# A DiT block on one core: summing the MLP gate over partition quadrants by small DMAs and VectorE in place of float32 matmuls between the fc1 panels

## The chip, the cores and the metric

The kernel runs on one core of one Trainium2 chip. The metric is device time in microseconds (us) of one execution. Each execution comes with the span of the core (first to last instruction; about 1.8 us less than the time) and the mean clock that the throttle granted TensorE. One execution of each kernel is profiled; its trace gives every instruction's start and duration.

## The reference

```python
B, N, D = 2, 256, 1152          # F = 4 * D, two heads
mod = (silu(c) @ w_mod).reshape(B, 6, 1, D)
shift_a, scale_a, gate_a, shift_m, scale_m, gate_m = [mod[:, i] for i in range(6)]
h = layernorm(x) * (1 + scale_a) + shift_a
...                                             # attention
x = x + gate_a * a
h2 = layernorm(x) * (1 + scale_m) + shift_m
m = gelu(h2 @ w_fc1) @ w_fc2
return x + gate_m * m
```

All inputs are bf16. The part that matters is the last line: `gate_m` is a vector of 1152 numbers for each of two batches, silu(c) times a 1152 x 1152 slice of `w_mod`, and it is needed only when fc2's results leave PSUM, the memory into which TensorE writes its sums.

## The kernel before

TensorE is the busy engine, so the kernel computes `gate_m` on VectorE. The rows of the weight slice lie on 128 partitions in 9 chunks; VectorE multiplies and adds the chunks, transposes 32x32 blocks and sums them. That leaves `folded`, whose 128 partitions are 4 quadrants of 32, still to be summed. The kernel before does this last sum with one float32 matmul for each batch against `fold`, which is four 32x32 identity matrices stacked. The two matmuls are issued on TensorE between the fc1 panels 34 and 35 (the last).

```python
fold = const.tile([P, 32], FP32, name="fold")
nc.vector.tensor_reduce(fold[:], ident[:].rearrange("p (q a) -> p a q", a=32), axis=AX.X, op=ALU.add)
# ...
def gate_vector(g, wg):
    # ... 18 passes of VectorE over 128 x 1152 make part
    for b in range(B):
        for c in range(0, D, PW):
            blocks = work.tile([P, PW // 32, 32], FP32, name="tmp", tag="tmp", bufs=3)
            nc.vector.transpose(blocks[:].rearrange("p j r -> p (j r)"), part[:, b, c:c + PW])
            nc.vector.tensor_reduce(folded[:, b, c // 32:(c + PW) // 32], blocks[:], axis=AX.X, op=ALU.add)
    return lambda: gate_vector_finish(g, folded)

def gate_vector_finish(g, folded):
    rows = D // 32
    pg = aux_tile([rows, B, 32], "pg")                       # PSUM
    for b in range(B):
        nc.tensor.matmul(pg[:, b, :], folded[:, b, :], fold[:], start=True, stop=True)
    nat = work.tile([rows, B, 32], BF16, name="nat_v", tag="nat_v", bufs=1)
    nc.vector.tensor_copy(nat[:], pg[:])
    for b in range(B):
        nc.gpsimd.dma_start(gates_dram[g, b, :].rearrange("(j r) -> j r", r=32), nat[:, b, :])
    return broadcast_gate(g)                                 # two DMAs: DRAM row -> all 128 partitions
# ... fc1, the panels of 128 columns of F from 12 on:
for m in range(MSPLIT, KF):                                  # MSPLIT = 12, KF = 36
    pacc = acc_tile([P, T], "pacc")                          # T = 512 tokens
    for k in range(KD):                                      # KD = 9
        f1_mm(pacc[:], m, k, 0, T, k == 0)
    nc.scalar.activation(gT[:, m, :], pacc[:], ACT.Gelu_apprx_tanh)
    if m == 22:
        gate_m_finish = gate_vector(1, w_gate_m)
    if m == KF - 2:
        gate_m = gate_m_finish()
    # ... fc2 weight loads
# ... fc2, 13 groups of 36 matmuls; each group's result is multiplied by the gate:
    nc.vector.tensor_tensor(tmp[:], pacc[:], gate_m[:, b, c0:c0 + cw], op=ALU.mult)
```

At the head, TensorE runs float32 matmuls on zeros only to warm up, `warm(2, pwarm)` and `warm(7, pwarm)`, until the first normalized rows of x arrive from VectorE (`norm1`).

## Time and profile before

| | before |
|---|---|
| time, median of three runs | 242.99 us (242.89 to 243.03) |
| span of the profiled execution | 241.3 us |
| TensorE matmul busy | 236.3 us, 98% |
| VectorE busy | 91.6 us, 38% |
| granted clock | 1.000 |

From the page of the kernel before, its first part (busy us, share of the span, count) and the split by engine of the chain that ended last (the waits and the work, followed back from the last instruction; a name with q is an engine's sequencer, and "issue" is time for which the profile shows no wait):

```profile
span 241.3 us, 3993 instructions
PE 236.3 (98%) x1698; PEld 144.6 (60%) x1698; DVE 91.6 (38%) x194; ACT 60.1 (25%) x122; POOL 28.3 (12%) x47
...
PE 95%; DMA 2%; DVE 1%; SPq 0%; issue 0%; DVEq 0%
```

TensorE is busy nearly all the time, and the chain of work that ended last runs on it for 95% of the span. So only what takes time away from TensorE, or makes it wait, changes the time.

The chain of the kernel before in order of time (start us, us, what):

```profile
1.63 4.60 DMA x_sb<-in_x_dram
...
9.37 0.53 PE pm L250 x18
...
97.31 68.26 PE pacc L750 x423
165.57 0.26 PE pg L491 x4
165.82 2.05 PE pacc L750 x9
167.87 70.31 PE pacc L806 x468
```

L750 is fc1, L806 is fc2. From 97.31 us on TensorE never waits. The gate appears in this chain for 0.26 us only, as pg. From the start of fc1 to the start of fc2 it is 167.87 - 97.31 = 70.56 us.

How long does pg hold TensorE up? From the timeline of the kernel before (start us, us, engine, line, operation; in brackets the idle time before it and who ended it):

```profile
163.66 0.60 ACT L782 ACTIVATE gT<-pacc 128x512 bf16<-128x512 f32 x1 [1.34 <-PE pacc L750]
165.50 0.21 PEld L491 LDWEIGHTS pg<-fold,folded 128*36 128x36 f32 x4 [0.42 <-issue]
165.50 0.33 PE L491 MATMUL pg<-fold,folded 128*36 128x32 f32 x4
165.61 0.60 ACT L782 ACTIVATE gT<-pacc 128x512 bf16<-128x512 f32 x1 [1.35 <-PE pacc L750]
165.76 2.12 PE L750 MATMUL pacc<-hT,w_f 128*128 128x512 bf16 x9
167.91 0.60 ACT L782 ACTIVATE gT<-pacc 128x512 bf16<-128x512 f32 x1 [1.71 <-PE pacc L750]
```

The Gelu of each panel starts when the panel is complete. Undisturbed panels follow each other at 1.94 us (163.66 to 165.61 within rounding); the last one takes 2.30 us. The difference of 0.36 us is what the two float32 matmuls (four passes) cost, with whatever they disturb around them.

### The profile page before, as it was taken

Reading aid. Unit: us, or ns where it says so; the run is one execution under the profiler, and the core shown is the slowest. Engines: PE = TensorE matmul, PEld = TensorE weight load, DVE = VectorE, ACT = ScalarE, POOL = GpSimd, SP = SyncE. Lnnn points to the kernel's source line nnn. Section 1 sums busy time; section 2 is a strip of 40 time slices with the busy share of each in tenths; the row PEclk is TensorE's granted clock in tenths of the full one; section 3 lists DMA queues with packets and bytes.
Section 4 is the critical chain, followed back from the end, with each engine's and each line's share of the span. In section 5 each row is a group of like instructions: output and inputs, shape, how many; then the busy total and the mean of one; then the engine's idle time right before and its main releaser. Section 6 shows DMA issues by size and latency. Waiting matters only on the chain.

```text
span 241.3 us, 3993 instructions
## 1 busy us (share of the span) xinstructions
PE 236.3 (98%) x1698; PEld 144.6 (60%) x1698; DVE 91.6 (38%) x194; ACT 60.1 (25%) x122; POOL 28.3 (12%) x47
## 2 busy tenths in 40 slices
PE   8899999999999999999999999999999999999994
PEld 5675444466667566888844444444666656666674
DVE  4842442319325678930002999950000000000001
ACT  6732322307215032770423333222000000000000
POOL 2300000001400324100000000001121111111111
PEclk9999999999999999999999999999999999999999
DMA  6999999998599994739999999999300000000000
GB/s 196 324 317 311 376 367 391 389 393 249 99 315 397 387 311 81 196 62 364 390 392 392 339 326 284 285 326 275 98 16 16 20 16 16 19 18 18 26 25 16
DMA packets 48925, 53.30 MB, mean 221 GB/s; under 512 B 9731, under 2 KB 36619, under 8 KB 48907
## 3 DMA queue, kind: packets, MB, share of 16 engines
q1 hardware_dynamic: 41312, 50.14, 62.6%
q10 hardware_dynamic: 7083, 1.72, 4.9%
q0 software_dynamic: 512, 1.19, 2.2%
q8 instruction: 13, 0.21, 0.4%
q14 instruction: 5, 0.04, 0.1%
HBM read 50.15 MB, written 1.19 MB: 213 GB/s over the span
## 4 chain that ended last, share of the span: by engine, by line
PE 95%; DMA 2%; DVE 1%; SPq 0%; issue 0%; DVEq 0%
PE pacc L806 29%; PE pacc L750 29%; PE pacc L697 7%; PE pacc L603 7%; PE pq L525 7%; PE pk L282 5%; PE pk L311 2%; DMA x_sb<-in_x_dram 2%; PE pa L644 2%; PE ps_s L560 2%; PE pn L420 2%; PE pt L267 1%; PE pm L250 1%; DVE stats L195 1%; PE pg L502 0%; SPq L88 0%
## 5 line engine op out<-in xcount | busy, mean ns | idle before, releaser
L750 PE MATMUL pacc<-hT,w_f 128*128 128x256 bf16 (+1 forms) x432 | 70.5, 326 | 0.0
L806 PE MATMUL pacc<-w_f,gT 128*128 128x384 bf16 (+2 forms) x468 | 70.5, 314 | 0.0
L806 PEld LDWEIGHTS <-gT 128*128 128x128 bf16 x468 | 44.4, 98 | 26.2
L750 PEld LDWEIGHTS <-w_f 128*128 128x128 bf16 x432 | 42.2, 98 | 27.6
L812 DVE TENSOR_TENSOR tmp<-pacc,gate 128x384 f32<-128x384 f32 (+2 forms) x13 | 6.9, 527 | 65.6 <-PE pacc L806 57.3
L782 ACT ACTIVATE gT<-pacc 128x512 bf16<-128x512 f32 x24 | 14.3, 597 | 32.7 <-PE pacc L750 32.7
L473 DVE SCALAR_TENSOR_TENSOR part<-w_gate_m,s,part 128x1152 f32<-128x1152 bf16 x16 | 21.4, 1414 | 0.0
L814 POOL TENSOR_TENSOR o_sb<-tmp,x 128x384 bf16<-128x384 f32 (+1 forms) x12 | 11.6, 971 | 53.9 <-DVE tmp L812 53.9
L697 PE MATMUL pacc<-w_o,big 128*128 128x384 bf16 x108 | 17.9, 326 | 0.0
L525 PE MATMUL pq<-hT,w_q 128*128 128x512 bf16 x81 | 17.8, 379 | 0.0
L603 PE MATMUL pacc<-w_v,hT 128*128 128x384 bf16 x108 | 17.7, 326 | 0.0
L603 PEld LDWEIGHTS <-hT 128*128 128x128 bf16 x108 | 10.5, 98 | 7.1 <-issue 0.3
L697 PEld LDWEIGHTS <-big 128*128 128x128 bf16 x108 | 10.4, 98 | 7.2 <-issue 0.4
L525 PEld LDWEIGHTS <-w_q 128*128 128x128 bf16 x81 | 7.9, 98 | 9.4
L282 PE MATMUL pk<-big,w_k 128*128 128x256 bf16 (+1 forms) x72 | 13.2, 325 | 0.0
L703 POOL TENSOR_TENSOR x<-tmp,x_sb 128x384 f32<-128x384 f32 x8 | 7.3, 911 | 26.3 <-DVE tmp L702 26.3
L471 DVE TENSOR_SCALAR part<-w_gate_m,s 128x1152 f32<-128x1152 bf16 x2 | 1.6, 818 | 22.2 <-DMA w_gate_m<-in_w_mod_dram 22.2
L495 POOL DMA_DIRECT2D gates_dram<-nat_v x2 | 1.1, 534 | 67.7 <-DVE nat_v L493 67.7
L282 PEld LDWEIGHTS <-w_k 128*128 128x128 bf16 x72 | 6.8, 97 | 3.5 <-issue 0.2
L771 ACT ACTIVATE gT<-pacc 128x512 bf16<-128x512 f32 x12 | 6.5, 597 | 9.1 <-PE pacc L750 9.1
L516 POOL DMA_DIRECT2D gates_dram<-nat x4 | 2.4, 596 | 49.8 <-DVE nat L513 48.4
L175 PE MATMUL pwarm<-zeros 128*128 128x256 f32 x18 | 6.7, 540 | 1.2 <-DVE eps_t L95 1.2
(106 smaller groups left out, 164.4 us busy)
## 6 DMA issues: line engine op xcount, KB each, us to landing
w_f<-in_w_fc_dram SPq DMA_DIRECT2D x12, 864.0 KB, 14.2
w_f<-in_w_fc_dram SPq DMA_DIRECT2D x3, 1728.0 KB, 10.1
w_f<-in_w_fc_dram SPq DMA_DIRECT2D x2, 2592.0 KB, 17.2
w_gate_a<-in_w_mod_dram SPq DMA_DIRECT2D x3, 864.0 KB, 14.4
w_v<-in_wqkv_dram SPq DMA_DIRECT2D x3, 864.0 KB, 15.4
w_o<-in_wo_dram SPq DMA_DIRECT2D x3, 864.0 KB, 14.7
w_shift_m<-in_w_mod_dram SPq DMA_DIRECT2D x3, 864.0 KB, 9.5
w_scale_m<-in_w_mod_dram SPq DMA_DIRECT2D x3, 864.0 KB, 15.8
```

The costliest lines, as they stand in the source:

```text
L175: nc.tensor.matmul(dst[:, 0:T // 2], zeros32[:, 0:P], zeros32, start=True, stop=True)
L282: nc.tensor.matmul(pk[m][:, c0:c1], w_k[:, k, m * P:(m + 1) * P], hT0[:, k, c0:c1], start=(k == 0 and c0 == 0), stop=(k == KD - 1), skip_g ...
L473: nc.vector.scalar_tensor_tensor(part[:, b, :], wg[:, k, :], s32[:, k, b:b + 1], part[:, b, :], op0=ALU.mult, op1=ALU.add,)
L525: nc.tensor.matmul(pq[m][:], w_q[:, k, m * P:(m + 1) * P], hT[:, k, :], start=(k == 0), stop=(k == KD - 1), skip_group_check=True,)
L603: nc.tensor.matmul(pacc[:], hT[:, k, t * P:(t + 1) * P], w_v[:, k, pnl * PW:(pnl + 1) * PW], start=(k == 0), stop=(k == KD - 1),)
L697: nc.tensor.matmul(pacc[:], aT[:, k, t * P:(t + 1) * P], w_o[:, k, c0:c1], start=(k == 0), stop=(k == KD - 1),)
L703: (nc.gpsimd if pool_add else nc.vector).tensor_tensor(x1[:, t, c0:c1], tmp[:], x_sb[:, t, c0:c1], op=ALU.add)
L750: nc.tensor.matmul(dst, w_f1[m // KD][:, k, ml * P:(ml + 1) * P], hT[:, k, c0:c1], start=start, stop=(k == KD - 1), **kw,)
L782: nc.scalar.activation(gT[:, m, :], pacc[:], ACT.Gelu_apprx_tanh)
L806: nc.tensor.matmul(pacc[:], gT[:, kk, t * P:(t + 1) * P], w_f2[j][:, r, c0 - n * PW:c0 - n * PW + cw], start=(kk == 0), stop=(kk == KF - 1),)
L812: nc.vector.tensor_tensor(tmp[:], pacc[:], gate_m[:, b, c0:c0 + cw], op=ALU.mult)
L814: (nc.vector if last else nc.gpsimd).tensor_tensor(o_sb[:], tmp[:], x1[:, t, c0:c0 + cw], op=ALU.add)
```

## The change

The intent: get the two float32 matmuls off TensorE. Four small DMAs bring the four quadrants side by side on 32 partitions, VectorE sums them, transposes, and converts to bf16, and the whole follows `folded` at once, without a place in TensorE's program.

```diff
-    fold = const.tile([P, 32], FP32, name="fold")
-    nc.vector.tensor_reduce(fold[:], ident[:].rearrange("p (q a) -> p a q", a=32), axis=AX.X, op=ALU.add)
 ...
-        return lambda: gate_vector_finish(g, folded)
-
-    def gate_vector_finish(g, folded):
         rows = D // 32
-        pg = aux_tile([rows, B, 32], "pg")
-        for b in range(B):
-            nc.tensor.matmul(pg[:, b, :], folded[:, b, :], fold[:], start=True, stop=True)
-        nat = work.tile([rows, B, 32], BF16, name="nat_v", tag="nat_v", bufs=1)
-        nc.vector.tensor_copy(nat[:], pg[:])
-        for b in range(B):
-            nc.gpsimd.dma_start(gates_dram[g, b, :].rearrange("(j r) -> j r", r=32), nat[:, b, :])
+        quads = small.tile([32, P // 32, B * rows], FP32, name="quads", tag="quads", bufs=1)
+        for a in range(P // 32):
+            nc.gpsimd.dma_start(quads[:, a, :], folded[32 * a:32 * (a + 1), :, :].rearrange("p b j -> p (b j)"))
+        total = small.tile([32, 96], FP32, name="total", tag="total", bufs=1)
+        nc.vector.memset(total[:], 0.0)
+        nc.vector.tensor_reduce(total[:, 0:B * rows], quads[:].rearrange("p a c -> p c a"), axis=AX.X, op=ALU.add)
+        turned = small.tile([32, 96], FP32, name="turned", tag="turned", bufs=1)
+        nc.vector.transpose(turned[:], total[:])
+        nat = small.tile([32, 96], BF16, name="nat_v", tag="nat_v", bufs=1)
+        nc.vector.tensor_copy(nat[:], turned[:])
+        # ... two DMAs of nat to gates_dram instead of two
         return broadcast_gate(g)
 ...
         if m == 22:
-            gate_m_finish = gate_vector(1, w_gate_m)
-        if m == KF - 2:
-            gate_m = gate_m_finish()
+            gate_m = gate_vector(1, w_gate_m)
```

More of the change, by code (lines that the diff above doesn't have):

```diff
@@ L483, in gate_vector @@
                 )
-        return lambda: gate_vector_finish(g, folded)
-    def gate_vector_finish(g, folded):
         rows = D // 32
-        pg = aux_tile([rows, B, 32], "pg")
-        for b in range(B):
-            nc.tensor.matmul(pg[:, b, :], folded[:, b, :], fold[:], start=True, stop=True)
-        nat = work.tile([rows, B, 32], BF16, name="nat_v", tag="nat_v", bufs=1)
-        nc.vector.tensor_copy(nat[:], pg[:])
-        for b in range(B):
-            nc.gpsimd.dma_start(gates_dram[g, b, :].rearrange("(j r) -> j r", r=32), nat[:, b, :])
+        quads = small.tile([32, P // 32, B * rows], FP32, name="quads", tag="quads", bufs=1)
[3 more added lines that the diff above has]
+        nc.vector.memset(total[:], 0.0)
+        nc.vector.tensor_reduce(
+            total[:, 0:B * rows], quads[:].rearrange("p a c -> p c a"), axis=AX.X, op=ALU.add,
+        )
+        turned = small.tile([32, 96], FP32, name="turned", tag="turned", bufs=1)
+        nc.vector.transpose(turned[:], total[:])
+        nat = small.tile([32, 96], BF16, name="nat_v", tag="nat_v", bufs=1)
+        nc.vector.tensor_copy(nat[:], turned[:])
+        flat = gates_dram[g, :, :].rearrange("b (j r) -> (b j) r", r=32)
+        nc.gpsimd.dma_start(
+            flat[0:64, :].rearrange("(q c) r -> c q r", q=2), nat[:, 0:64].rearrange("c (q r) -> c q r", q=2),
+        )
+        nc.gpsimd.dma_start(flat[64:B * rows, :], nat[0:B * rows - 64, 64:96])
         return broadcast_gate(g)
```

## The prediction

> **What bounds the kernel now.** TensorE. The page's first part shows PE busy 236.3 of 241.3 us (98%), and the chain of waits is 95% PE. The clock is 1.000. In the fc1/fc2 stretch the chain is PE without a gap: 68.26 us of fc1 panels, then "PE pg L491 0.26 us", then 2.05 us of the last panel, then 70.31 us of fc2. So of the MLP gate only those matmuls are on the critical path.
>
> **What the change removes.** (a) The four float32 matmul passes of pg between panels 34 and 35. Two ways to cost them: the chain gives 0.26 us; the spacing of the Gelu starts is 1.94 us for every panel from 12 on, and 2.30 us (165.61 to 167.91) for the panel with pg in front of it. The difference, 0.36 us, also holds the drain and the restart of the weight loads, so I take 0.36 us. [...] a 128x36 float32 load takes 114 ns, a 128x128 bf16 load 98. (b) One VectorE reduction (fold, 0.36 us at 32.8 us), with VectorE idle 4.8 us afterwards: worth nothing.
>
> **What it adds.** The order of instructions shows nothing moved on TensorE or ScalarE. Four small DMAs on GpSimd's queue once folded is ready (160.4 us), then on VectorE a memset, a 32x288 reduction, a 32x96 transpose and a copy, then two small DMAs instead of two. Both engines are idle there, so this delays nobody.
>
> **When the gate arrives.** Before: nat_v DMAs issued at 166.4 and 166.9 (0.53 us each, landing in 3.5 to 3.8 us), broadcast from 170.8, and the first fc2 multiply starts at 174.40, waiting for that DMA. After: four issues from about 160.7 to 162.9, landing about 166 to 166.5 (the weight loads still move some 315 GB/s there); VectorE about 0.9 us (estimated from the 553 ns reduction of 384 columns and the 317 ns transpose of 128); two DMAs to about 171; broadcast to about 175.5. [...] this trace has 3.5 to 3.8, and I use the trace. The first fc2 group ends near 173.5, so its multiply waits 1 to 4 us. This is off the path: there are six PSUM accumulators and a group lasts 5.9 us, so TensorE would stall for the gate only if it came near 200 us.
>
> **Predicted time.** 242.99 - 0.36 = 242.6 us, 0.15% faster, just above the 0.14 us scatter of the three runs. Range 242.3 to 242.95. Chances: faster by over 2% 0.003, within 2% 0.994, slower 0.003.
>
> **What would show each step.** Right: no pg matmuls, 1.94 us between all the last Gelu starts, fc2 starting 0.35 us earlier (167.35 instead of 167.71), PE busy time down 0.3 us, quads landing near 166, first fc2 multiply at 174 to 177.5 with a wait for the gate DMA, no wait of PE in fc2. Wrong: an fc2 matmul waiting for VectorE; a shift of the fc1 start (97.1 us).
>
> **What would make it wrong.** Small DMAs stuck behind the weight loads for over 20 us; a lower granted clock; a shift in the first 30 us, where DMA bounds the kernel, from other placement of tiles or semaphores, which would hide a gain of this size.

Two clauses are cut where marked; no term of the sum went with them, and 242.99 - 0.36 = 242.6 us stands.

## The result, and the profile after

| | before | after |
|---|---|---|
| six executions each, median | 243.01 us (242.89 to 243.35) | 243.32 us (242.89 to 244.04) |
| ratio, after over before | | 1.0013, 95% interval 0.9997 to 1.0028 |
| span of the profiled execution | 241.3 us | 241.4 us |
| start of fc1 to start of fc2, from the chain | 70.56 us | 70.20 us |

A ratio here is the mean time of one kernel's runs over that of the other's runs of the same rounds; it is not quite the ratio of the medians. Executions over 1.5% slower than the fastest of the same kernel are left out of the means.

Within 2%, as forecast. But the time lies above the forecast range, and if anything the change looks slower. The page of the changed kernel, the same lines:

```profile
span 241.4 us, 3993 instructions
PE 235.1 (97%) x1694; PEld 144.0 (60%) x1694; DVE 92.2 (38%) x196; ACT 60.2 (25%) x122; POOL 30.3 (13%) x51
...
PE 95%; DMA 3%; SPq 1%; DVE 0%; issue 0%; DVEq 0%
```

TensorE has four matmul passes fewer and is busy 1.2 us less (0.3 was forecast), yet the span is 0.1 us longer. The busy time says little of the gain here: 0.8 of the 1.2 us is the warming at the head, which ended at 7.14 us and not at 7.95. The chain of the changed kernel (L755 is fc1 now, L809 fc2):

```profile
2.58 7.20 DMA w_scale_a<-in_w_mod_dram
...
9.82 0.60 PE pm L250 x18
...
97.80 70.20 PE pacc L755 x432
168.00 70.30 PE pacc L809 x468
```

Here is the whole result in two subtractions. From the start of fc1 to the start of fc2: 168.00 - 97.80 = 70.20 us, against 70.56, so 0.36 us less, to the last digit what was forecast. But fc1 starts at 97.80 us and not at 97.31: 0.49 us later. At the head of the chain stands another load: the first piece of w_scale_a kept TensorE waiting until 9.82 us, where in the kernel before these matmuls stand at 9.37. The change has no instruction there. The gain is real in its stage, and was lost 88 us before that stage began.

The timeline of the changed kernel around the last panels and the gate:

```profile
161.53 2.02 POOL L486 DMA_DIRECT2D quads<-folded  x4 [62.38 <-DVE total L488]
...
164.15 0.60 ACT L787 ACTIVATE gT<-pacc 128x512 bf16<-128x512 f32 x1 [1.35 <-PE pacc L755]
166.09 0.60 ACT L787 ACTIVATE gT<-pacc 128x512 bf16<-128x512 f32 x1 [1.34 <-PE pacc L755]
...
168.04 0.60 ACT L787 ACTIVATE gT<-pacc 128x512 bf16<-128x512 f32 x1 [1.35 <-PE pacc L755]
168.63 0.63 DVE L489 TENSOR_REDUCE total<-quads 32x72 f32<-32x288 f32 x1 [7.30 <-DMA quads<-folded]
...
175.69 0.56 DVE L815 TENSOR_TENSOR tmp<-pacc,gate 128x384 f32<-128x384 f32 x1 [5.89 <-DMA gate<-gates_dram]
```

The last Gelus are 1.94 us apart now, the last one too. The gate arrives at 175.69 us (174.40 before, forecast 175.5), and VectorE is idle for 5.89 us before it. The first fc2 group is complete at 173.85 us, so the gate alone accounts for 1.84 us of that, within the forecast 1 to 4. TensorE does not notice: fc2 takes 70.30 us as before.

So what has to be explained is the 0.49 us at the start. Three theories:

- S: the landing of the first loads scatters from one execution to the next, in both kernels alike; the first comparison was unlucky.
- L: the change moves something. It does: without `fold`, every large tile stands 128 bytes lower in SBUF, the on-chip memory for tiles (128 bytes a partition is the size of `fold`; the addresses were read from the built programs, which the kept traces do not show), among them the targets of the first loads.
- a third, that the cost on TensorE was misread and something else hides it.

### The profile page after: what moved, and what is told of

The parts are those of the page before. It is cut to its first block, busy times and chain, and to the rows that moved or that the text cites. A ratio compares the mean times of both kernels' runs of the same rounds, so it can differ in the third digit from the quotient of the medians.

```text
span 241.4 us, 3993 instructions
## 1 busy us (share of the span) xinstructions
PE 235.1 (97%) x1694; PEld 144.0 (60%) x1694; DVE 92.2 (38%) x196; ACT 60.2 (25%) x122; POOL 30.3 (13%) x51
## 4 chain that ended last, share of the span: by engine, by line
PE 95%; DMA 3%; SPq 1%; DVE 0%; issue 0%; DVEq 0%
PE pacc L809 29%; PE pacc L755 29%; PE pacc L702 7%; PE pacc L608 7%; PE pq L530 7%; PE pk L282 5%; DMA w_scale_a<-in_w_mod_dram 3%; PE pk L311 2%; PE pa L649 2%; PE ps_s L565 2%; PE pn L420 2%; PE pt L267 1%; PE pm L250 1%; SPq L88 1%; PE pg L507 0%
## 5 line engine op out<-in xcount | busy, mean ns | idle before, releaser
L809 PE MATMUL pacc<-w_f,gT 128*128 128x384 bf16 (+2 forms) x468 | 70.5, 314 | 0.0
L755 PE MATMUL pacc<-hT,w_f 128*128 128x256 bf16 (+1 forms) x432 | 70.4, 326 | 0.0
L809 PEld LDWEIGHTS <-gT 128*128 128x128 bf16 x468 | 44.4, 98 | 26.2
L755 PEld LDWEIGHTS <-w_f 128*128 128x128 bf16 x432 | 42.3, 98 | 27.8
L486 POOL DMA_DIRECT2D quads<-folded x4 | 2.0, 509 | 62.4 <-DVE total L488 62.4
L707 DVE TENSOR_TENSOR tmp<-pacc,gate 128x384 f32<-128x384 f32 x12 | 6.6, 549 | 3.1 <-PE pacc L702 3.1
```

The costliest lines, as they stand in the source:

```text
L707: nc.vector.tensor_tensor(tmp[:], pacc[:], gate_a[:, b, c0:c1], op=ALU.mult)
L755: nc.tensor.matmul(dst, w_f1[m // KD][:, k, ml * P:(ml + 1) * P], hT[:, k, c0:c1], start=start, stop=(k == KD - 1), **kw,)
L809: nc.tensor.matmul(pacc[:], gT[:, kk, t * P:(t + 1) * P], w_f2[j][:, r, c0 - n * PW:c0 - n * PW + cw], start=(kk == 0), stop=(kk == KF - 1),)
```

## The experiments

Eighteen runs were made, in five calls, each on another chip and with its own eleven executions of the kernel before.

### First call: repeat, move the tiles, take only the matmuls out

**e1_after_again**: the changed kernel, no edit.

> The changed kernel once more, unaltered. Theory S (scatter of the start: the landing of the first x and w_scale_a loads varies by about half a us from one execution to the next, the same in both kernels): mean of the rounds about 0.36 us under the kernel before, 242.6 to 242.9, and in its profile the fc1 start may lie anywhere from 97.2 to 97.9 us while fc1 start to fc2 start stays 70.20 us. Theory L (placement: dropping the fold tile moves every large tile by 128 bytes in SBUF, and the first loads land later for it, always): about 243.3 again, fc1 start near 97.8 us.

Measured: its profiled execution (276.94 us, mean granted clock 0.853; its clock record has 0.850 from 5.05 us to the end) is left out. The five others: 242.57 to 243.51 us, mean 242.99; the kernel before in the same rounds 243.41; ratio 0.9982 (0.9964 to 0.9999). Theory S expected a mean 0.36 us below the kernel before and got 0.42; theory L expected 243.3. So the changed kernel is not always slower. But the kernel before, measured eleven times, ran between 242.84 and 243.91: the scatter is far over the 0.14 us of the first three runs.

**e2_after_fold**: the changed kernel with `fold` back, so the large tiles stand where they stood.

```diff
+    fold = const.tile([P, 32], FP32, name="fold")
+    nc.vector.tensor_reduce(fold[:], ident[:].rearrange("p (q a) -> p a q", a=32), axis=AX.X, op=ALU.add)
```

> The changed kernel with the unused fold tile and its reduction put back, so that x_sb, w_scale_a, w_k and all large tiles stand at the addresses of the kernel before; the float32 matmuls stay away. Theory L: the start is again that of before (fc1 start 97.3 us) and the whole gain shows: 242.6 us, ratio to before 0.9985. Theory S: no different from e1_after_again within the scatter, whatever that is.

Measured: mean 242.87 us (242.62 to 242.98), ratio 0.9977 (0.9963 to 0.9991). That is 0.12 us under e1, well inside the scatter.

**e3_before_layout**: the kernel before with the large tiles where the changed kernel has them.

```diff
-    fold = const.tile([P, 32], FP32, name="fold")
+    fold = small.tile([P, 32], FP32, name="fold", tag="fold", bufs=1)
...
-        nat = work.tile([rows, B, 32], BF16, name="nat_v", tag="nat_v", bufs=1)
+        nat = small.tile([rows, B, 32], BF16, name="nat_v", tag="nat_v", bufs=1)
```

> The kernel before with fold and nat_v moved to the other pool, so that all large tiles stand at the addresses of the changed kernel; the same instructions, the float32 matmuls stay. Theory L: fc1 start near 97.8 us, 243.5 us, ratio 1.002. Theory S: as before, 243.0 us, ratio 1.000 within 0.1%.

Measured: mean 243.56 us (243.27 to 243.79) against 243.41, ratio 1.0007 (0.9991 to 1.0023). fc1 started at 97.57 us in its chain. The time itself fits what theory L had written, 243.5, but only because the kernel before was at 243.41 in these rounds too and not at 243.0; the ratio is what counts, and it is a third of the 1.002 expected. Moving the tiles down cost 0.15 us here and moving them up gained 0.12 in e2. Neither is clear of noise, and the upper end of e3's interval, 1.0023, is still 0.56 us. Taken together the two give 0.14 us with a standard error of 0.11 from the spread of their times: an effect of 0.1 us cannot be excluded, but the 0.5 us that theory L needed is unlikely. A trace speaks against it too: e7 below, which has the tiles where the kernel before has them, waited for the same piece of w_scale_a until 9.90 us, longer than the changed kernel did (9.82).

**e4_before_nopg**: the kernel before with only the matmuls gone. Its output is wrong, which doesn't matter for the time.

```diff
-        pg = aux_tile([rows, B, 32], "pg")
-        for b in range(B):
-            nc.tensor.matmul(pg[:, b, :], folded[:, b, :], fold[:], start=True, stop=True)
...
-        nc.vector.tensor_copy(nat[:], pg[:])
+        nc.vector.tensor_copy(nat[:], folded[0:rows, :, 0:32])
```

> The kernel before with only the four float32 matmul passes taken out (nat_v is copied from folded itself, so the MLP gate is wrong on purpose); layout, fold reduction and DMAs as before. Both theories, if the cost of the matmuls on TensorE was read rightly: fc1 start to fc2 start 70.20 us instead of 70.56, and 242.65 us, ratio 0.9985. If the gain is not there even so, the cost of the matmuls was misread.

Measured: mean 243.04 us (242.42 to 244.01), ratio 0.9983 (0.9962 to 1.0005). Its chain:

```profile
97.23 70.20 PE pacc L747 x432
167.43 70.30 PE pacc L803 x468
```

70.20 us again, with layout and DMAs as before. The price of the matmuls on TensorE is 0.36 us, and nothing of the added DMAs or VectorE work takes any of it back.

### What all traces agree on

The table takes each trace of a fast execution with the usual head of the program and no matmuls added, and reads five starts from it: TensorE's first matmul of the k projection, of the q projection, of fc1, of fc2, and the end. These are starts of instructions; the chain counts a piece from the end of the one before, which is some 0.16 us later.

| trace | pg on TensorE | first k | first q | first fc1 | first fc2 | end | fc1 to end |
|---|---|---|---|---|---|---|---|
| before | yes | 10.13 | 31.92 | 97.15 | 167.71 | 241.26 | 144.12 |
| e15_before_look | yes | 9.96 | 31.71 | 96.94 | 167.50 | 241.05 | 144.12 |
| e3_before_layout | yes | 10.44 | 32.17 | 97.40 | 167.97 | 241.52 | 144.12 |
| after | no | 10.64 | 32.40 | 97.64 | 167.84 | 241.39 | 143.76 |
| e12_after_third | no | 10.12 | 31.86 | 97.09 | 167.29 | 240.85 | 143.76 |
| e16_after_look | no | 9.99 | 31.70 | 96.93 | 167.13 | 240.69 | 143.76 |
| e2_after_fold | no | 10.13 | 32.19 | 97.43 | 167.63 | 241.18 | 143.75 |
| e4_before_nopg | no | 10.10 | 31.84 | 97.07 | 167.27 | 240.82 | 143.75 |
| e11_gate_late | no | 9.97 | 31.71 | 96.94 | 167.14 | 240.69 | 143.75 |

The last column has two values, 144.12 with the matmuls and 143.75 or 143.76 without. From the first q matmul to the first fc1 matmul it is 65.23 or 65.24 us in every row. All the variation is in the first 32 us: the first q matmul lies anywhere from 31.70 to 32.40 us, twice the size of the gain.

In e2_after_fold the start has a second source of delay: its k projection began as early as in the kernel before, but its chain then runs through the load of w_q:

```profile
20.29 11.85 DMA w_q<-in_wqkv_dram
32.14 0.04 issue
32.19 5.35 PE pq L532 x24
```

TensorE could not start q before that load landed.

### Second call: delay the start, multiply the cost

**e5_late_before** and **e6_late_after**: both kernels with more warming, so that TensorE comes to the first loads later.

```diff
-    warm(7, pwarm)
+    warm(14, pwarm)
```

> The kernel before with seven more warming matmuls at the head of TensorE's program, so that TensorE reaches the first projection some 3 us later, when the first x and w_scale_a tiles have landed in every execution. Theory S (the disputed sign of the change is scatter of the first landings): slower than before by 2 to 4 us, and its executions lie within about 0.3 us of each other, where those of the kernel before spread over 1.1 us; fc1 start to the end stays 144.12 us. Theory L (the placement, not scatter): the spread stays as it is.

> The changed kernel with the same seven matmuls. Theory S: 0.36 us under e5_late_before in the mean of the rounds, with little scatter, so that the gain is seen in the whole time and not only in the stage; fc1 start to the end 143.76 us. Theory L: as slow as e5_late_before or slower, since its large tiles stand 128 bytes lower.

Measured: e5 mean 244.77 us (244.27 to 245.30), e6 mean 244.75 us (244.01 to 245.32). The scatter did not shrink and the difference of the means is 0.02 us. Expectation missed. In their traces the stage still has its two values, 144.12 and 143.75 us. These runs seemed to speak against theory S; the third call showed why they could not tell.

**e7_pg12_f32**: the kernel before with twelve more pairs of float32 matmuls of pg's shape, one pair after each of twelve panels. **e8_pg12_bf16**: the same pairs in bf16.

```diff
+    px = aux_tile([36, B, 32], "px")
     for m in range(MSPLIT, KF):
 ...
+        if KF - 14 <= m < KF - 2:
+            for e in range(B):
+                nc.tensor.matmul(px[:, e, :], shift_m[:].rearrange("p k c -> p (k c)")[:, 0:36], fold[:], start=True, stop=True)
```

(in e8 the two operands are `ident[:, 0:36]` and `ident[:, 0:32]`)

> The kernel before with twelve more pairs of float32 matmuls of pg's shape, one pair after each of panels 22 to 33, results unused. If the price of one pair between two panels is 0.36 us, as the spacing of the Gelu starts says: 12 x 0.36 = 4.3 us more, about 247.4 us, ratio 1.018, and each of those panels 2.30 us instead of 1.94. If it is the 0.26 us of the chain: 3.1 us more. If the matmuls cost TensorE nothing in truth: no change.

> The same with twelve pairs of bf16 matmuls of the same shape. If the price is mostly that of float32 (four passes and slower weight loads instead of two): under half of e7_pg12_f32, about 0.1 to 0.15 us a pair, 1.2 to 1.8 us more. If it is mostly a drain of TensorE at any odd matmul between the panels: nearly as much as e7_pg12_f32.

Measured: e7 mean 247.47 us (247.15 to 247.91), ratio 1.0166; e8 mean 246.52 us (245.95 to 247.01), ratio 1.0127. The kernel before had a mean of 243.42 us in these rounds, so twelve float32 pairs cost 4.05 us of whole time (4.3 expected). In the trace of e7, fc1 to the end is 148.44 us, 4.32 us over 144.12: 0.36 us a pair. Multiplied by twelve, the cost is far above the scatter. From the timeline of e7:

```profile
163.46 0.33 PE L790 MATMUL px<-fold,shift_m 128*36 128x32 f32 x4
163.56 0.60 ACT L783 ACTIVATE gT<-pacc 128x512 bf16<-128x512 f32 x1 [1.71 <-PE pacc L750]
...
165.76 0.33 PE L790 MATMUL px<-fold,shift_m 128*36 128x32 f32 x4
165.87 0.60 ACT L783 ACTIVATE gT<-pacc 128x512 bf16<-128x512 f32 x1 [1.71 <-PE pacc L750]
```

163.56 to 165.87: every panel with a pair in front of it takes 2.30 us. The 0.26 us that the chain had given for pg was too small; the spacing of what follows is the better measure.

In e8 fc1 to the end is 147.14 us, which is 3.02 us over 144.12, so 0.25 us for a bf16 pair. Neither expectation fits: 0.25 is 70% of the float32 price. So most of the price of an odd pair of tiny matmuls is the break in the stream of panels, and 0.11 us is what float32 adds. Each float32 matmul counts as two passes in the trace, so pg makes four.

The starts of the matmuls show where the price is paid. In the undisturbed stream they are 216 ns apart. From the last matmul ahead of a pair to the second one after it, the steps are 309, 40, 108 and 226 ns for bf16, and 309, 56, 35, 35, 132 and 226 ns for float32, in e7 and around pg itself in the kernel before. What exceeds 216 in the outer two, plus the inner ones, makes 0.25 and 0.36 us. The chain's 0.26 us for pg is the inner steps alone; 0.10 us, the same for both types, lies in the matmuls around them.

### Third call: a long delay, a late gate, one more repeat

**e9_later_before**, **e10_later_after**: as e5 and e6 with `warm(54, pwarm)`.

> The kernel before with 47 more warming matmuls, some 20 us, at the head of TensorE's program. Seven did not shrink the scatter, so the first landings alone are not its source. Theory D (all scatter comes from loads landing in the first 32 us, the first tiles or those of w_q, and TensorE waiting for them): with 20 us of lead every load of that stretch has landed, and the executions lie within 0.3 us of each other. Theory E (the scatter arises elsewhere, in the stages from the q projection on, or in the clock): the spread stays about 1 us.

> The changed kernel with the same 47. Theory D: 0.36 us under e9_later_before in the mean, with a scatter of under 0.3 us, so the difference is clear of noise. Theory E: about 0.36 us under it in the mean as well, but lost in a spread of 1 us. Theory L (placement): not faster than e9_later_before.

Measured: e9 mean 262.30 us (261.57 to 263.09), e10 mean 261.36 us (261.16 to 261.79); ratios to the kernel before 1.0773 and 1.0735. The scatter of e9 is 1.5 us, wider than before, and that of e10 0.63 us, so theory D as stated missed for both. The chains show what was wrong with the experiment. e9:

```profile
3.37 24.96 PE pwarm L175 x108
28.33 0.45 PE pt L267 x8
```

and e10:

```profile
3.37 24.28 PE pwarm L175 x108
27.65 0.45 PE pt L267 x8
```

The same 108 warming passes took 24.96 us in one execution and 24.28 in the other. TensorE starts at half speed (a pass of this size every 0.43 us) and steps up to full speed (every 0.22 us); in the 18 traces of executions at ordinary speed the clock record has the step anywhere from 4.44 to 7.60 us (4.44 in the changed kernel, 6.08 in the kernel before), a range of 3.16 us. What sets its time was not shown. In the traces of the unaltered kernels but one the warming ends before VectorE delivers the first rows, and the step is hidden. (The one is e16: its step came at 7.58 us, and the warming that ended at 8.69 stands in its chain, but its first k matmul, at 9.99 us, is among the earliest.) In e5, e6, e9 and e10 the warming sits on the critical path, so they carry this scatter in place of that of the loads. They are void as a test of S; the 0.94 us between the means of e9 and e10 must not be read as the gain: of the 1.13 us between their two profiled executions, 0.68 is this. For the executions that were not traced it is not shown.

**e11_gate_late**: the changed kernel with 24 passes of useless VectorE work ahead of the gate's transposes.

```diff
+        for i in range(24):
+            nc.vector.tensor_scalar_mul(part[:, i % B, :], part[:, i % B, :], 1.0)
```

> The changed kernel with 24 multiplications of part by 1.0 on VectorE ahead of the transposes, some 16 to 19 us, so that the gate lands near 193 us instead of 175.7. If the gate's arrival is off the critical path with slack to about 200 us: time as the changed kernel without them, no TensorE wait in fc2, and fc2 70.3 us long. If there is no such slack: up to 17 us slower.

Measured: mean 242.83 us (242.45 to 243.49), ratio 0.9974 (0.9957 to 0.9991); fc1 to the end 143.75 us. The gate reached VectorE at 187.03 us, earlier than the 193 intended, but 11.3 us later than in the changed kernel:

```profile
187.03 1.49 DVE L817 TENSOR_TENSOR tmp<-pacc,gate 128x384 f32<-128x384 f32 x3 [5.97 <-DMA gate<-gates_dram]
190.81 0.56 DVE L817 TENSOR_TENSOR tmp<-pacc,gate 128x384 f32<-128x384 f32 x1 [2.30 <-PE pacc L811]
```

Three groups had queued up (x3); the next waits for TensorE again, and the time is unchanged. So the gate's path has at least 11 us of slack beyond the changed kernel's. Where exactly the slack ends was not tried.

**e12_after_third**: the changed kernel, no edit.

> The changed kernel once more, unaltered, on one more chip. If the gain is 0.36 us in a spread of 1 us: mean of its rounds 0.1 to 0.7 us under the kernel before, ratio 0.9975 to 0.9995, with an interval that may hold 1. If the change costs something outside the trace of the MLP: above 1.

Measured: mean 243.00 us (242.45 to 243.89), the kernel before 243.42; ratio 0.9981 (0.9961 to 1.0001). The same 0.42 us as in e1.

### Fourth and fifth call: hold the start by VectorE's clock

A better way to fix the start is to let VectorE hold it, whose durations hardly vary (the hold below takes 6.26 us in each of the traces of e13, e14 and e18), with the warming over before the hold ends.

**e13_held_before**, **e14_held_after**:

```diff
-    warm(7, pwarm)
+    warm(22, pwarm)
 ...
+    hold = kT.rearrange("p k t -> p (k t)").bitcast(FP32)
+    for _ in range(8):
+        nc.vector.tensor_scalar_mul(hold[:, 0:D], x_sb[:, 1, :], 1.0)
     norm1(1, 0, CUT)
```

> The kernel before with eight multiplications on VectorE (0.82 us each in the gate's first pass, 6.5 us) ahead of the first normalization, and 15 more warming matmuls that end before it: the first projection starts 5 to 6.5 us later, by VectorE's clock, after the first loads have landed and TensorE has reached its full speed. Theory D (the scatter is the landing of the early loads, 0.75 us in the traces so far, and of TensorE's step up in speed): 248 to 249.5 us and the executions within 0.3 us of each other. Theory E (it arises elsewhere): spread about 1 us as in the kernel before.

> The changed kernel with the same hold. Theory D: 0.36 us (0.25 to 0.45) under e13_held_before, executions within 0.3 us, so the intervals of the two do not overlap. Theory E: the same mean difference in a spread of 1 us. Theory L (placement costs the gain): no difference or slower.

Measured: e13 mean 249.06 us (248.89 to 249.37, five runs), e14 mean 248.89 us (248.52 to 249.24, six runs). The scatter is down, 0.48 and 0.72 us wide, not to 0.3; the difference is 0.17 us and the sets overlap, so the 0.25 to 0.45 us expected of e14 was missed. Two flaws show in the traces. The warming still ended last (15.17 us, the step to full speed coming at 7.6 us in both), and e14's trace has a wait that no other trace has. Its chain before fc1:

```profile
99.30 3.21 DMA hT<-xn
...
105.66 1.72 ACTq L694
107.39 0.05 issue
107.43 0.61 ACT hT L672
108.04 0.04 issue
108.08 19.37 PE pacc L758 x175
```

A step of the second layer norm on ScalarE, queued behind the issue of a transpose by DMA, held fc1 for 0.24 us: fc1 to the end is 144.00 us here, 143.75 or 143.76 in every other fast trace without pg. (ACTq is ScalarE's sequencer.)

**e15_before_look** and **e16_after_look**: the two kernels unaltered, one profiled execution each.

> The kernel before, unaltered, for one more trace of its start. fc1 start to the end 144.12 us; the whole varies with the start of the first projection alone, 9.9 to 10.8 us so far, later still if this is one of the executions over 243.8 us.

> The changed kernel, unaltered, for one more trace of its start. fc1 start to the end 143.75 us; the whole varies with the start of the first projection alone.

Measured: 242.84 us and 242.46 us, each a single run; their starts are in the table. The first k matmul was at 9.96 and 9.99 us, the earliest of the unaltered kernels. No trace of an unaltered kernel is of an execution above 243.3 us, so the slowest ones were never seen from inside.

**e17_held19_before**, **e18_held19_after**: as e13 and e14, with `warm(19, pwarm)`.

> As e13_held_before with 3 fewer warming matmuls (1.3 us), so that VectorE's hold alone sets the start. Theory D (most of the scatter is the start): 248.3 to 248.9 us, executions within 0.4 us of each other. Theory E (a large part arises later, as in the late transpose seen in e14_held_after): a spread of 0.7 us or more remains.

> As e14_held_after with 3 fewer warming matmuls. Theory D: 0.36 us (0.25 to 0.45) under e17_held19_before, with a scatter of at most 0.4 us. Theory E: a mean difference between 0 and 0.6 us in a spread of 0.7 us or more. Theory L (placement costs the gain): no difference or slower.

Measured: e17's profiled execution was pathological (1441.2 us, TensorE some six times slower throughout, 11.86 us for a panel of 1.94) and is left out. The view of the cores shows a clock of 1.000 for it, but its trace holds no clock record, so that 1.000 is no measurement. Its four others: 250.24 to 250.54 us, mean 250.36, with granted clocks of 0.991 to 0.993. e18's six: 248.51 and 248.56 us with granted clocks of 0.999 and 1.000, and 249.82 to 250.14 us, mean 249.95, with 0.991 to 0.993. The trace of one of the latter shows what such a clock is. Three stretches of it (their length, the busy time of PE, PEld, DVE, ACT and POOL, then the granted clock, the DMA share and GB/s):

```profile
12.80:16.20 3.40, 1.59 (x33) 1.21 (x32) 2.63 (x7) 0.50 (x2) 0.56 (x2) 1.00 1.15 318
16.20:19.60 3.40, 3.40 (x21) 2.52 (x19) 2.02 (x9) 0.84 (x2) 0.00 (x0) 0.50 1.19 301
19.60:23.00 3.40, 3.40 (x46) 2.90 (x44) 1.55 (x6) 0.84 (x2) 0.00 (x0) 1.00 1.10 323
```

and its timeline before that:

```profile
14.88 0.29 PE L267 MATMUL pt<-ident,xn 128*128 128x128 bf16 x2 [1.81 <-DVE xn L235]
```

TensorE was idle for 1.81 us, and a little later the granted clock was 0.50 for one stretch of 3.4 us (16.20 to 19.61 us in the clock record). In the stretch before it, the first of the three, TensorE was busy for 1.59 of 3.40 us, 47%. That the idle time brought on the half speed is the reading of this one trace; how much idle time it takes was not shown. One such stretch costs about 1.4 us (estimated from e18's executions, 249.95 against 248.5). With three warming matmuls fewer, eight of the ten executions at ordinary speed had a granted clock of 0.991 to 0.993, where those of e13 and e14 had 0.998 to 1.000; one of the eight was traced. So the hold brought in a third kind of scatter, and the 248.3 to 248.9 us expected of e17 was missed. Comparing only executions of the same kind, those with granted clock 0.991 to 0.993: 249.95 against 250.36, a difference of 0.41 us, and the two sets do not overlap (at most 250.14 against at least 250.24). This grouping was made after seeing the runs.

The unaltered kernel before has one such execution among 61: 244.80 us at a granted clock of 0.993. That a half-speed stretch caused it is likely from its clock; it was not traced.

### All executions together

| | runs | mean | range |
|---|---|---|---|
| before: first comparison | 6 | 243.05 | 242.89 to 243.35 |
| before: five later calls | 55 | 243.41, 243.42, 243.42, 243.50, 243.47 | 242.81 to 244.80 |
| after: first comparison | 6 | 243.36 | 242.89 to 244.04 |
| after: e1, e12, e16 | 12 | 242.99, 243.00, 242.46 | 242.45 to 243.89 |

All fast runs of the kernel before: 61, mean 243.41 us, standard deviation 0.40. Of the changed kernel: 18, mean 243.09, standard deviation 0.47: 0.32 us less, with a standard error of 0.12 worked out from these deviations. With the variants whose head is the usual one put in as well (e3 with pg; e2, e4 and e11 without) it is 67 runs at 243.42 against 36 at 243.00: 0.42 us less, standard error 0.09. So a gain of about 0.36 us is there in the whole time, if the executions are taken as independent. This pooling was chosen after the runs.

## Why the prediction was right or wrong

**The price of the matmuls, 0.36 us: right.** Fc1 start to fc2 start went from 70.56 to 70.20 us, the last Gelu spacing from 2.30 to 1.94; removing nothing but the matmuls (e4) gives the same 70.20, and twelve more pairs cost 12 x 0.36 us in the trace (e7). The other estimate that the prediction had put beside it, 0.26 us from the chain, was too small, as the prediction supposed.

**What it called the reason, partly.** It named the drain and the restart of the weight loads. The starts in the trace of the kernel before show both: in the undisturbed stream a weight load starts 1 or 2 ns after the start of the matmul ahead of it, pg's first load 308 ns after (165.499 against 165.191 us), and the panel's next load 128 ns after pg's last matmul (165.754 against 165.626). Beside them it put the float32 weight load, 114 ns for 128x36 against 98 for 128x128 in bf16. The bf16 pairs of e8 cost 0.25 us each, so float32 is 0.11 us of the 0.36; the rest is breaking into the stream of large matmuls at all.

**Nothing on the path is delayed by the added work: right.** Fc2 takes 70.30 us with no TensorE wait in the chain, and 11 us more of delay (e11) does not change that.

**The arrival of the gate: right in the sum by luck, wrong in the parts.** Forecast 175.5, measured 175.69 us; two errors cancelled. The four quadrant DMAs took 5.3 us each to land and not about 3.7, since they ran while fc2's weights were loading (322 GB/s from 161.5 to 168.6 us); the two that followed took 1.6 us and not 3.5 or more, since by then the loading was done (2 GB/s from 170.1 to 172.6 us). With the gate made late (e11), quadrant DMAs without that traffic (11 GB/s) landed in 1.6 us. The last line of the view of the tile quads, for the changed kernel and for e11:

```profile
DMA to landing us min/median/max: 5.3/5.3/5.4
...
DMA to landing us min/median/max: 1.5/1.6/1.6
```

**The time and its range: wrong.** The step that failed is this one: "242.99 - 0.36 = 242.6 us, 0.15% faster, just above the 0.14 us scatter of the three runs. Range 242.3 to 242.95". The second term was right. The first was not the kernel's time but the median of three executions that happened to lie close together and low. Sixty-one executions of the kernel before have a mean of 243.41 us and range over 2.0 us. The forecast with these numbers would have been 243.41 - 0.36 = 243.05 us, with 0.5 us to either side for eight in ten single executions (1.3 times 0.40); the 18 executions of the changed kernel have a mean of 243.09. The prediction took three agreeing runs for a measure of scatter. Of the signs that it had set itself, the stage showed its own, but fc2 started at 167.84 us and not at 167.35, because fc1 had started at 97.64, a shift that it had listed as a sign of being wrong.

**"A shift in the first 30 us, where DMA bounds the kernel": it came, but not from the cause it named.** From 4 to 30 us the DMA share was 1.09 in the trace of the kernel before (326 GB/s) and 1.08 in that of the changed one, while TensorE was busy for 25.29 and 24.00 of the 26.00 us; so DMA is seen to bound this stretch only where the chain goes through a load (4.60 us before, 7.20 after, and 11.85 of w_q in e2). The two profiled executions differ by 0.49 us before fc1, all of it before the first q matmul. The prediction put it down to "other placement of tiles or semaphores". Moving the tiles either way (e2, e3) gave 0.12 and 0.15 us, inside the noise. In the traces the start differs between executions of one and the same kernel (the changed one: first q matmul at 31.70, 31.86 and 32.40 us), by when the first loads land.

**What stays open.** In the first comparison the changed kernel was 0.31 us slower on average, 0.67 us away from the later finding. For two sets of six at a standard deviation of 0.40 the standard error is 0.23 us, so this is close to three of them: chance is the simplest reading, since e1 and e12 did not repeat it, but it is not shown. Three of the six times of the kernel before there are the very ones that the prediction had, and the record does not name the chip. Where the executions above 243.5 us lose their time is not shown either, as none of them was traced; late first loads, a late w_q and a late second layer norm were each seen in some trace and could do it. A half-speed stretch like e18's could not, save in the one of 244.80 us: it takes 0.007 off the mean clock (e18), and all the others have 0.998 or more. The experiments point to no version that beats both kernels clearly; e2 has the lowest mean of the correct ones with the usual head besides e11, by less than the noise.

## What to carry to other kernels

Three runs that agree within 0.1% do not say that the scatter is 0.1%: before forecasting or claiming a third of a microsecond, measure the kernel as it is ten times or more, and on more than one chip. When the gain is smaller than the scatter, read it from the stage, between two events that both kernels share (here first fc1 matmul to the end: two values in nine traces), and confirm the size by multiplying the cost until it stands clear of the noise. An experiment that delays the start to hide one source of scatter can put another on the path, so look at its trace before believing its times.
